# Spreading the first weight loads of a decode block over two hardware DMA queues

## The chip, the cores and the metric

The kernel runs on one core of a Trainium2 chip. The metric is device time in microseconds (us), the median of several executions. Executions of the kernel before agree within about 0.1%, so differences of half a microsecond can be discussed but are near the noise. The profile covers one execution; its span (421.8 us for the kernel before) is about 1.9 us shorter than the measured device time. In the text, MB is 10^6 bytes. The 2048 KB of one K, V or wq load are 2.10 MB, the 1536 KB of one wmod load 1.57 MB. The engines go by their names in the profile: PE multiplies matrices (PEld loads its weights), DVE, ACT and POOL compute on vectors, and SP (SyncE) issues transfers. A load is issued by an engine, waits in a queue, is moved by the DMA engines, and lands when all its bytes are there.

## The reference, cut to what matters

```python
mod = (_silu(c) @ w_mod).reshape(c.shape[0], 6, 1, -1)   # w_mod: 1024 x 6144, 12.6 MB
h = _layernorm(x) * (1 + ca) + sa                        # ca, sa: two of the six parts of mod
q = h @ wq                                               # wq: 1024 x 4096, 8.4 MB
scores = q . k_cache * Dh**-0.5                          # 2 x 4 x 32768 x 128 keys, 67 MB
o = softmax(scores) @ v_cache                            # the same number of values, 67 MB
x = x + ga * (o @ wo)
x = x + gb * MLP(layernorm(x) * (1 + cb) + sb)           # w1, w2, 7.3 MB each; wo is 8.4 MB
```

There are only two rows of x, one per batch. Every weight, key and value is read once: about 178 MB for very little arithmetic per byte.

## The kernel before

All big loads form one ordered list, the stream, and `need(key)` issues it up to the item asked for. SBUF gives the stream a 160 KB ring per partition. Where a load overwrites an older item, its issue waits until the PE has read that item (`frees`):

```python
for k in range(KT8):                                   # 8 slices of w_mod, rows of 12 KB
    add(("wmod", k), [6 * DM], wm_v[:, k, :], k * 12 * KB)
for k in range(4):                                     # 4 loads of wq, rows of 8 KB
    add(("wq", k), [2, HQ * D], ..., (96 + 16 * k) * KB)
for cc in range(4):
    add_kv("K", 0, cc)                                 # K0..K3 of the first of 8 rounds, rows of 16 KB
...                                                    # then V and the next round's K, and so on
def need(*key):
    it = by_key[key]
    while pos[0] <= it.n:
        cur = stream[pos[0]]
        old = [...]                                    # items whose bytes this one overwrites
        ...
        T.dma("sp", lambda e, ...: e.dma_start(dst, src), key=cur.sem, writes=[cur.reg], frees=old)
        pos[0] += 1
    return it
```

`"sp"` is the SyncE instruction stream, so every load goes through that engine's one hardware queue. The start of the kernel is:

```python
need("wmod", 0)
T.dma("sp", ... c2 <- c ...)
T.dma("sp", ... x16 <- A_x ...)
...
for k in range(KT8):                 # PE turns c into columns
    pe(matmul(psM, c2, ident))
act(activation(sgT, cv, ACT.Sigmoid))
...                                  # layernorm of x
for k in range(KT8):
    it = need("wmod", k)             # 12 matmuls for each slice of w_mod
...                                  # modT, modulate
for k in range(KT8):
    it = need("wq", k // 2)          # 8 matmuls for each half of a wq load
...                                  # qT; then the rounds over K and V begin
```

Below, sgT is the sigmoid of c, modT the product with w_mod and qT the query, each turned into columns.

K0 and K1 of the first round overwrite wmod 0 to 2, K2 overwrites wmod 5 and 6, K3 overwrites wq 0. The K0 of the second round overwrites the first round's K0, so it can't be issued before the PE has transposed that tile, and the transposes stand after the q matmuls in the PE's program.

Of the kernel before, what the change touches and what calls it, by code (L numbers as in the profile page):

```python
# [255 lines left out]
def bass_adaLN_cond__gqa_block_cached__mixer_channel_mlp__decode_kernel(  # L256
# [15 lines left out]
    T = Tracker(nc)  # L272
# [133 lines left out]
# [4 lines that stand above are left out]
            old = [o.reg for o in stream[:cur.n] if o.off < cur.off + cur.nbytes and cur.off < o.off + o.nbytes]  # L410
            if len(cur.view.shape) == 3:
                dst = cur.view[:, :, :]
            else:
                dst = cur.view[:, :]
            T.dma("sp", lambda e, dst=dst, src=cur.src: e.dma_start(dst, src), key=cur.sem, writes=[cur.reg], frees=old)  # L415
            pos[0] += 1
        return it

# [7 lines left out]
    def pe(fn, reads=(), writes=(), mark=True):  # L426
        T.inst("pe", fn, reads=reads, writes=writes, mark=mark, sem="pl" if T.lag else None)

    need("wmod", 0)
    T.dma("sp", lambda e: e.dma_start(c2[:, :], c), key="ld_c", writes=["KT_sb0"])  # L430
    T.dma("sp", lambda e: e.dma_start(x16[:, :], A_x.rearrange("b o (k p) -> (b o k) p", p=128)), key="ld_x", writes=["x16"])

    for t, nm in ((ident, "ident"), (identf, "identf")):
        T.inst("pool", lambda e, t=t: e.memset(t[:, :], 0.0), writes=[nm])
# [52 lines left out]
    for k in range(KT8):  # L487
        it = need("wmod", k)
        for ch in range(12):
            n, q = ch // 4, ch % 4  # L490
            pe(lambda e, w=it.view, k=k, ch=ch, n=n, q=q: e.matmul(bank[n][32 * q:32 * q + 32, :], lhsT=inT[:, k, :], rhs=w[:, ch * 512:(ch + 1) * 512],  # L491
                                                                   start=(k == 0), stop=(k == KT8 - 1), skip_group_check=True),
               reads=[it.reg, "inT"], writes=[breg[n]], mark=(ch % 4 == 3))
    for n in range(3):
        dst = row[:, n * 512:(n + 1) * 512]
# [12 lines left out]
    for k in range(KT8):  # L508
        it = need("wq", k // 2)
        for ch in range(8):  # L510
            n, q = ch // 4, ch % 4
            pe(lambda e, w=it.view, k=k, ch=ch, n=n, q=q: e.matmul(bank[n][32 * q:32 * q + 32, :], lhsT=inT[:, k, :], rhs=w[:, k % 2, ch * 512:(ch + 1) * 512],  # L512
                                                                   start=(k == 0), stop=(k == KT8 - 1), skip_group_check=True),
               reads=[it.reg, "inT"], writes=[breg[n]], mark=(ch % 4 == 3))
# [286 lines left out]
```

## Time and profile before

| | kernel before |
|---|---|
| median of device time | 423.67 us (423.66 to 423.82, 3 runs) |
| span of the profile | 421.8 us |
| bytes read | 178.28 MB |
| busy: PE, ACT, DVE | 71%, 37%, 40% |
| first bytes move, last load lands | about 1.5 us, 416.0 us |

From the page of the kernel before: the DMA engines' busy share in forty slices, what they moved, the data queue (packets, MB, share of the 16 engines' span), the bytes read, and the chain that ended last by engine.

```profile
DMA  8999999999999999999999999999999999999995
GB/s 334 429 431 423 435 432 423 429 432 426 433 432 429 435 429 430 435 429 429 435 429 432 437 423 433 435 426 433 433 428 433 430 430 435 427 429 424 428 423 244
...
q1 hardware_dynamic: 14322, 178.29, 99.1%
...
HBM read 178.28 MB, written 0.00 MB: 423 GB/s over the span
...
DMA 80%; PE 16%; ACT 2%; SPq 1%; issue 0%; DVE 0%
```

The rate is flat from the second slice to the last but one, whatever the compute engines do in the meantime. That is the sign of a kernel bound by its bytes. The 80% of DMA in the chain must be read with care. The chain counts a transfer from its issue to its landing, and most of that time is spent in the queue. The view of the K tiles gives that time:

```profile
DMA to landing us min/median/max: 20.2/31.6/35.7
```

A K tile alone takes 2.10 MB / 430 GB/s = 4.9 us (an estimate from the measured rate). So a tile that lands 31.6 us after its issue had some five tiles ahead of it. This is slack: the issue could have come later, and the engines would still have had work.

The timeline of the kernel before, cut to the landmarks at the start (start in us, duration in us, engine, line, operation, output<-input; SPq is SyncE's issuing of loads):

```profile
0.74 0.39 SPq L415 DMA_DIRECT2D wmod<-in_w_mod_dram  x1
...
1.93 3.45 SPq L415 DMA_DIRECT2D wmod<-in_w_mod_dram  x7
...
5.42 16.82 SPq L415 DMA_DIRECT2D wq<-in_A_wq_dram  x4
...
7.60 0.18 ACT L446 ACTIVATE sgT<-psM 128x16 f32<-128x16 f32 x1 [5.59 <-PE psM L444]
...
10.44 1.04 PE L491 MATMUL psS<-wmod,inT 128*32 128x512 bf16 x8
...
22.28 21.50 SPq L415 DMA_DIRECT2D K<-in_A_k_cache_dram  x4
...
40.57 0.26 DVE L506 COPY modT<-psM 128x96 f32<-128x96 f32 x1 [5.38 <-PE psM L503]
...
56.49 0.23 DVE L522 CAST qT<-psM 128x64 bf16<-128x64 f32 x1 [0.54 <-PE psM L519]
...
65.08 11.90 SPq L415 DMA_DIRECT2D K<-in_A_k_cache_dram  x3
```

Seven wmod issues took 3.45 us, but the four wq issues took 16.82 us. Nothing in the program makes wq wait, so the queue itself held SyncE back. The last two lines show the second round: its K0 is issued at 65.08 us, 8.6 us after qT. The windows of the kernel before show that none of this left the DMA engines without work after the first few us. Each line gives the window and its length in us, the busy time (and count of instructions) of PE, PEld, DVE, ACT and POOL, the clock granted to the PE, the busy share of the DMA engines (1 is all of them, all the time) and GB/s:

```profile
0.00:10.00 10.00, 1.33 (x12) 1.18 (x12) 1.20 (x7) 2.75 (x3) 3.34 (x15) 1.00 0.83 329
10.00:50.00 40.00, 22.82 (x170) 9.55 (x170) 3.73 (x14) 0.80 (x2) 0.00 (x0) 1.00 1.01 428
50.00:90.00 40.00, 28.99 (x560) 26.11 (x557) 17.79 (x28) 15.14 (x18) 0.38 (x2) 0.93 1.01 431
```

### The profile page before, as it was taken

Reading aid. Unit: us, or ns where it says so; the run is one execution under the profiler, and the core shown is the slowest. Engines: PE = TensorE matmul, PEld = TensorE weight load, DVE = VectorE, ACT = ScalarE, POOL = GpSimd, SP = SyncE. Lnnn points to the kernel's source line nnn. Section 1 sums busy time; section 2 is a strip of 40 time slices with the busy share of each in tenths; the row PEclk is TensorE's granted clock in tenths of the full one; section 3 lists DMA queues with packets and bytes.
Section 4 is the critical chain, followed back from the end, with each engine's and each line's share of the span. In section 5 each row is a group of like instructions: output and inputs, shape, how many; then the busy total and the mean of one; then the engine's idle time right before and its main releaser. Section 6 shows DMA issues by size and latency. Waiting matters only on the chain.

```text
span 421.8 us, 11638 instructions
## 1 busy us (share of the span) xinstructions
PE 299.5 (71%) x5171; PEld 238.1 (56%) x5171; DVE 167.1 (40%) x347; ACT 156.6 (37%) x269; POOL 6.0 (1%) x31
## 2 busy tenths in 40 slices
PE   1547478878997688587877848796888682445576
PEld 1105158866975678476767828684776671112244
DVE  1102026644663476155534724652474352101311
ACT  2000025547645349142833633383447245000020
POOL 3000000000000000000000000000000000000000
PEclk9999999969989999796988997898899696655565
DMA  8999999999999999999999999999999999999995
GB/s 334 429 431 423 435 432 423 429 432 426 433 432 429 435 429 430 435 429 429 435 429 432 437 423 433 435 426 433 433 428 433 430 430 435 427 429 424 428 423 244
DMA packets 14335, 178.47 MB, mean 423 GB/s; under 512 B 1513, under 2 KB 1520, under 8 KB 2802
## 3 DMA queue, kind: packets, MB, share of 16 engines
q1 hardware_dynamic: 14322, 178.29, 99.1%
q8 instruction: 9, 0.15, 0.1%
q14 instruction: 4, 0.03, 0.0%
HBM read 178.28 MB, written 0.00 MB: 423 GB/s over the span
## 4 chain that ended last, share of the span: by engine, by line
DMA 80%; PE 16%; ACT 2%; SPq 1%; issue 0%; DVE 0%
DMA K<-in_A_k_cache_dram 60%; PE psKT L542 11%; DMA wo<-in_A_wo_dram 8%; DMA w<-in_B_w_dram 7%; DMA wmod<-in_w_mod_dram 4%; PE psS L554 3%; ACT E_sb L575 1%; PE psO L584 1%; SPq L415 1%; ACT KT_sb L546 1%; PE psO L757 1%; PE psS L678 0%; ACT L575 0%; PE psM L565 0%; ACT S_sb L558 0%
## 5 line engine op out<-in xcount | busy, mean ns | idle before, releaser
L542 PE MATMUL psKT<-ident,K 128*128 128x128 bf16 x2048 | 173.8, 237 | 39.0 <-DMA K<-in_A_k_cache_dram 37.8
L542 PEld LDWEIGHTS psKT<-ident,K 128*128 128x128 bf16 x2048 | 133.2, 106 | 49.7 <-DMA K<-in_A_k_cache_dram 44.9
L548 DVE COPY KT_sb<-psKT 128x1024 bf16<-128x1024 bf16 x160 | 108.3, 689 | 112.5 <-PE psKT L542 112.5
L546 ACT ACTIVATE KT_sb<-psKT 128x1024 bf16<-128x1024 bf16 x96 | 98.0, 1020 | 131.2 <-PE psKT L542 131.2
L554 PE MATMUL psS<-qcur,KT_sb 128*128 128x8 bf16 x2048 | 88.2, 167 | 8.1 <-ACT KT_sb L546 6.7
L554 PEld LDWEIGHTS psS<-qcur,KT_sb 128*128 128x128 bf16 x2048 | 79.5, 99 | 13.2 <-ACT KT_sb L546 8.1
L584 PE MATMUL psO<-V,E_sb 128*32 128x512 bf16 x512 | 35.5, 403 | 6.3 <-DMA V<-in_A_v_cache_dram 5.0
L575 ACT ACTIVATE E_sb<-S_sb,negm 128x256 bf16<-128x256 f32 x64 | 32.3, 504 | 7.7 <-DVE negm L571 6.8
L559 DVE TENSOR_REDUCE m1c<-psS 128x8 f32<-128x512 f32 x32 | 22.1, 691 | 14.4 <-ACT S_sb L558 13.3
L558 ACT ACTIVATE S_sb<-psS 128x512 f32<-128x512 f32 x32 | 19.0, 592 | 14.1 <-PE psS L554 14.1
L584 PEld LDWEIGHTS psO<-V,E_sb 128*32 128x32 bf16 x512 | 11.5, 100 | 16.8 <-DMA V<-in_A_v_cache_dram 5.7
L491 PE MATMUL psS<-wmod,inT 128*32 128x512 bf16 x64 | 8.4, 622 | 11.9 <-DMA wmod<-in_w_mod_dram 11.9
L678 PE MATMUL psS<-wo,atT 128*32 128x512 bf16 x64 | 7.6, 627 | 11.3 <-DMA wo<-in_A_wo_dram 11.3
L462 ACT ACTIVATE stat<-stat 128x2 f32<-128x2 f32 x3 | 0.6, 204 | 38.9 <-DVE stat L461 38.9
L512 PE MATMUL psS<-wq,inT 128*32 128x512 bf16 x64 | 7.6, 627 | 6.9 <-DMA wq<-in_A_wq_dram 5.9
L575 ACT ACTIVATION_READ_ACCUMULATOR E_sb<-S_sb,negm 128x1 f32 x64 | 12.1, 189 | 0.0
L491 PEld LDWEIGHTS psS<-wmod,inT 128*32 128x32 bf16 x64 | 1.3, 112 | 17.9 <-DMA wmod<-in_w_mod_dram 17.4
L678 PEld LDWEIGHTS psS<-wo,atT 128*32 128x32 bf16 x64 | 1.9, 128 | 16.3 <-DMA wo<-in_A_wo_dram 10.3
L604 PE MATMUL psM<-msum,hmat 128*128 128x128 f32 x16 | 4.4, 359 | 7.1 <-DVE msum L599 7.1
L497 ACT ACTIVATE S_sb<-psS 128x512 f32<-128x512 f32 x1 | 0.6, 597 | 22.8 <-DVE S_sb L499 22.8
L499 DVE COPY S_sb<-psS 128x512 f32<-128x512 f32 x1 | 0.7, 692 | 20.6 <-PE psS L491 20.6
L599 DVE SCALAR_TENSOR_TENSOR msum<-psO,mk,msum 128x128 f32<-128x128 f32 x24 | 8.4, 351 | 0.8
(116 smaller groups left out, 132.3 us busy)
## 6 DMA issues: line engine op xcount, KB each, us to landing
K<-in_A_k_cache_dram SPq DMA_DIRECT2D x32, 2048.0 KB, 31.6
V<-in_A_v_cache_dram SPq DMA_DIRECT2D x32, 2048.0 KB, 35.1
wmod<-in_w_mod_dram SPq DMA_DIRECT2D x8, 1536.0 KB, 16.5
wq<-in_A_wq_dram SPq DMA_DIRECT2D x4, 2048.0 KB, 37.5
wo<-in_A_wo_dram SPq DMA_DIRECT2D x4, 2048.0 KB, 29.0
w<-in_B_w_dram SPq DMA_DIRECT2D x4, 1792.0 KB, 39.1
w<-in_B_w_dram SPq DMA_DIRECT2D x3, 2048.0 KB, 30.6
w<-in_B_w_dram SPq DMA_DIRECT2D x1, 768.0 KB, 28.0
```

Source lines behind the costliest of these rows:

```text
L491: pe(lambda e, w=it.view, k=k, ch=ch, n=n, q=q: e.matmul(bank[n][32 * q:32 * q + 32, :], lhsT=inT[:, k, :], rhs=w[:, ch * 512:(ch + 1) * 512],
L512: pe(lambda e, w=it.view, k=k, ch=ch, n=n, q=q: e.matmul(bank[n][32 * q:32 * q + 32, :], lhsT=inT[:, k, :], rhs=w[:, k % 2, ch * 512:(ch + ...
L542: pe(lambda e, kq=kq, jj=jj, w=it.view, t=t: e.transpose(psKT[kq][:, jj * 128:(jj + 1) * 128], w[:, t, :], ident[:, :]), reads=[it.reg, "i ...
L546: act(lambda e, src=src: e.activation(KT_sb[g8][:, :, :], src, ACT.Copy), reads=[f"psKT{kq}"], writes=[f"KT_sb{g8}"], sem=f"ev{cc}_{g8}")
L548: dve(lambda e, src=src: e.tensor_copy(KT_sb[g8][:, :, :], src), reads=[f"psKT{kq}"], writes=[f"KT_sb{g8}"], sem=f"ev{cc}_{g8}")
L554: pe(lambda e, t=t, jj=jj: e.matmul(ps[:, t * HPG:(t + 1) * HPG], lhsT=KT_sb[g8][:, jj, :], rhs=qcur[:, :], start=True, stop=True), reads= ...
L558: act(lambda e: e.activation(Sc, ps[:, :].rearrange("p (t h) -> p h t", h=HPG), ACT.Copy), reads=[preg], writes=[f"S_sb{i % 2}_{cc}"], sem ...
L559: dve(lambda e: e.tensor_reduce(m1c[:, :, cc], ps[:, :].rearrange("p (t h) -> p h t", h=HPG), AX.X, ALU.max), reads=[preg], writes=[f"m1c{ ...
L575: act(lambda e: e.activation(E_sb[:, :, h, :], S_sb[j][:, h, :].rearrange("p (u t) -> p u t", t=4), ACT.Exp, bias=negm[:, h:h + 1], scale= ...
L584: pe(lambda e, t4=t4, tg=tg, q=q: e.matmul(psO[32 * q:32 * q + 32, :], lhsT=E_sb[:, tg // 4, :, :].rearrange("p h t -> p (h t)"), rhs=it.v ...
L599: dve(lambda e, q=q: e.scalar_tensor_tensor(out=msum[:, :], in0=psO[:, q * 128:(q + 1) * 128], scalar=mk4[:, q:q + 1], in1=msum[:, :], op0 ...
L678: pe(lambda e, w=it.view, g=g, j=j, hf=hf, q=q: e.matmul(psS[0][32 * q:32 * q + 32, :], lhsT=atT[g][:, j, :], rhs=w[:, j, hf * 512:(hf + 1 ...
```

## The change

The intent is to let two instruction streams issue the first twelve loads: odd slices of wmod and odd loads of wq go through ACT's hardware queue, the others stay on SyncE's. The early call of `need("wq", 3)` puts ACT's six issues at the head of its program, ahead of its sigmoid.

```diff
+            E = "act" if cur.key[0] in ("wmod", "wq") and cur.key[1] % 2 else "sp"
-            T.dma("sp", lambda e, ...: e.dma_start(dst, src), key=cur.sem, ...)
+            T.dma(E, lambda e, ...: e.dma_start(dst, src), key=cur.sem, ...)
...
     need("wmod", 0)
     T.dma("sp", ... c2 <- c ...)
     T.dma("sp", ... x16 <- A_x ...)
+    need("wq", 3)
```

More of the change, by code (lines that the diff above doesn't have):

```diff
@@ L414, in need @@
                 dst = cur.view[:, :]
-            T.dma("sp", lambda e, dst=dst, src=cur.src: e.dma_start(dst, src), key=cur.sem, writes=[cur.reg], frees=old)
+            E = "act" if cur.key[0] in ("wmod", "wq") and cur.key[1] % 2 else "sp"
+            T.dma(E, lambda e, dst=dst, src=cur.src: e.dma_start(dst, src), key=cur.sem, writes=[cur.reg], frees=old)
             pos[0] += 1
```

## The prediction

> **What bounds the kernel now.** The stream of bytes. The page counts 178.28 MB read in a 421.8 us span; its forty slices show the DMA engines 0.9 busy or more in all but the first and the last. In ten-microsecond windows the rate is 420 to 439 GB/s from 10 to 410 us, although PE, ACT and DVE are often half idle. 178.28 MB at 430 GB/s would be 415 us; the rest is the start (nothing moves before 1.5 us; half-microsecond windows show 123, 295, 369 and 393 GB/s from 2 to 4 us, 418 after) and the tail from the last landing (416.0 us). The chain of waits names DMA for 80%, but most of that is queueing: a K tile lands 31.6 us (median) after its issue, never sooner than 20.2 us, V never sooner than 17.9 us, while 2.1 MB at 430 GB/s take 4.9 us (estimate). So 10 us of lateness in an issue costs nothing.
>
> **What the change removes, adds, moves.** Bytes and arithmetic stay. Six issues (wmod 1, 3, 5, 7, wq 1, 3) move from SP to the head of ACT's program.
> - SP's timeline shows about 0.46 us per issue while its queue has room, then 3.07, 6.36 and 6.82 us for wq 1 to 3: back-pressure. These stalls should shrink. They cost nothing today: the engines are full behind them.
> - ACT pays about 6 x 0.46 = 2.8 us at the start, where it only waits for c (5.6 us idle before its sigmoid at 7.6 us). If ACT's queue stalls too, the sigmoid is late but PE catches up: one wmod slice takes it 1.3 us, against 3.65 us to load.
> - Landings: the queues share the engines, so slices should land in pairs. c and x, behind wmod 0, land near 10 us instead of 6.9; first wmod matmul about 13.5 us instead of 10.4. wmod 6 and 7 land together near 32 us; the modT copy moves from 40.6 to about 41.5 us. wq 2 and 3 land together near 53 us; the qT copy moves from 56.5 to about 58.5 us. K0 still lands near 58 us.
>
> The Trainium skill ("DMA: Bandwidth & Descriptors", section "Issuing engines are not separate DMA queues") says loads issued from different engines run on the same 16 DMA engines and interleave, saving only sequencer issue time. The trace of before has one data queue and can't show this.
>
> **How much is critical.** The issue stalls: 0. The lateness of modT and qT: 0, since it delays the issues of K3 (43.5 us now) and of the second round's K0 (65.1 us), each with over 10 us of transfers queued ahead. A fuller start may win: the deficit against 430 GB/s from 1.5 to 4 us is about 0.8 us (estimate from the windows), of which a second queue may fill a quarter. Mixing two queues over 21 MB could change the rate by 1% either way, 0.5 us.
>
> **Predicted: 423.5 us, range 422.7 to 424.4. Chances: faster by over 2% 0.01, within 2% 0.97, slower by over 2% 0.02.**
>
> **What would show the steps.** A second hardware queue with about 10.5 MB, total unchanged; 425 to 435 GB/s from 10 to 50 us; wmod landings in pairs about 7.3 us apart; first wmod matmul 3 us later, modT about 1 us, qT about 2 us later; SP's wq stalls much shorter; K0 lands within 1.5 us of 58 us; from 90 us on both traces agree to about 1 us.
>
> **What would make it wrong.** Two queues mixing clearly below 430 GB/s; one queue served so unfairly that a slice lands 15 us late and K3 is issued into an empty queue; ACT blocked for over 25 us at its issues; a start-up gain above 1 us.

## The result, and the profile after

| | before | after |
|---|---|---|
| median | 423.67 us (423.61 to 423.82, 4 runs) | 423.75 us (423.6 to 423.91, 4 runs) |
| span of the profile | 421.8 us | 421.9 us |
| ratio after / before | | 1.0002, 95% interval 0.9984 to 1.0019 |

A ratio here is the mean time of one kernel's runs over that of the other's of the same rounds, so it isn't quite the ratio of the medians. The time did not change.

The same lines of the page of the changed kernel (q10 is the queue of ACT):

```profile
DMA  8999999999999999999999999999999999999995
GB/s 330 431 429 422 434 433 424 426 433 426 430 437 426 435 432 426 435 435 426 433 433 427 437 428 430 437 426 430 437 426 435 432 427 434 433 424 424 427 426 244
...
q1 hardware_dynamic: 13202, 167.80, 93.3%
q10 hardware_dynamic: 1120, 10.49, 5.9%
...
HBM read 178.28 MB, written 0.00 MB: 423 GB/s over the span
...
DMA 74%; PE 20%; ACT 3%; issue 2%; SPq 1%; DVE 1%; DVEq 0%
```

The second queue, q10, is there with 10.49 MB. The total and the rate are the same. The timeline of the changed kernel (ACTq is ACT's issuing of loads):

```profile
0.73 1.94 ACTq L416 DMA_DIRECT2D wmod<-in_w_mod_dram  x4
...
2.70 1.09 ACTq L416 DMA_DIRECT2D wq<-in_A_wq_dram  x2
...
3.46 1.06 SPq L416 DMA_DIRECT2D wq<-in_A_wq_dram  x2
...
12.21 0.18 ACT L448 ACTIVATE sgT<-psM 128x16 f32<-128x16 f32 x1 [7.10 <-PE psM L446]
...
15.04 1.04 PE L493 MATMUL psS<-wmod,inT 128*32 128x512 bf16 x8
...
17.84 28.30 SPq L416 DMA_DIRECT2D K<-in_A_k_cache_dram  x4
...
42.83 0.26 DVE L508 COPY modT<-psM 128x96 f32<-128x96 f32 x1 [5.38 <-PE psM L505]
...
58.29 0.22 DVE L524 CAST qT<-psM 128x64 bf16<-128x64 f32 x1 [0.55 <-PE psM L521]
...
66.22 12.17 SPq L416 DMA_DIRECT2D K<-in_A_k_cache_dram  x3
```

The issue stalls on wq are gone: 16.82 us for four before, 1.09 and 1.06 us for two and two now. SyncE then issued the first K0 at 17.84 us instead of 22.28, but K0 stood behind the same bytes: by the time from issue to landing of that one load (35.7 us before, 40.2 us now) it landed at 58.0 us in both kernels. In exchange the compute of the start is later: the sigmoid by 4.6 us, the first wmod matmul by 4.6 us, modT by 2.3 us, qT by 1.8 us, the second round's K0 by 1.1 us. The windows of the changed kernel:

```profile
0.00:10.00 10.00, 0.00 (x0) 0.00 (x0) 0.00 (x0) 1.28 (x1) 3.33 (x15) 1.00 0.83 325
10.00:50.00 40.00, 21.81 (x165) 11.17 (x165) 4.92 (x21) 2.27 (x4) 0.00 (x0) 1.00 1.01 428
50.00:90.00 40.00, 30.51 (x587) 26.95 (x588) 18.36 (x31) 15.64 (x18) 0.38 (x2) 0.83 1.01 429
```

The stretch in which two queues mix (10 to 50 us) moved bytes at 428 GB/s in both kernels. The last load's matmuls start at 416.09 us, against 416.02 us before.

### The profile page after: what moved, and what is told of

Its sections match the earlier page's. It is cut to its first block, busy times and chain, and to the rows that moved or that the text cites. A ratio compares the mean times of both kernels' runs of the same rounds, so it can differ in the third digit from the quotient of the medians.

```text
span 421.9 us, 11638 instructions
## 1 busy us (share of the span) xinstructions
PE 298.1 (71%) x5171; PEld 239.6 (57%) x5171; DVE 167.5 (40%) x347; ACT 156.8 (37%) x269; POOL 6.0 (1%) x31
## 3 DMA queue, kind: packets, MB, share of 16 engines
q10 hardware_dynamic: 1120, 10.49, 5.9%
## 4 chain that ended last, share of the span: by engine, by line
DMA 74%; PE 20%; ACT 3%; issue 2%; SPq 1%; DVE 1%; DVEq 0%
DMA K<-in_A_k_cache_dram 47%; PE psKT L544 13%; DMA wq<-in_A_wq_dram 12%; DMA wo<-in_A_wo_dram 8%; DMA w<-in_B_w_dram 7%; PE psS L556 4%; ACT E_sb L577 1%; PE psO L586 1%; SPq L416 1%; ACT KT_sb L548 1%; PE psS L514 1%; PE psO L759 1%; PE psS L680 0%; ACT L577 0%; ACT S_sb L560 0%
## 5 line engine op out<-in xcount | busy, mean ns | idle before, releaser
L586 PE MATMUL psO<-V,E_sb 128*32 128x512 bf16 x512 | 34.6, 396 | 3.6 <-DMA V<-in_A_v_cache_dram 2.1
L561 DVE TENSOR_REDUCE m1c<-psS 128x8 f32<-128x512 f32 x32 | 22.1, 691 | 14.3 <-ACT S_sb L560 13.1
L514 PEld LDWEIGHTS psS<-wq,inT 128*32 128x32 bf16 x64 | 2.4, 139 | 10.8 <-DMA wq<-in_A_wq_dram 6.6
L444 PE MATMUL psM<-ident,KT_sb 2*128 2x2 bf16 x8 | 0.6, 194 | 11.1 <-DMA KT_sb<-in_c_dram 11.1
```

Of the source, the lines that this page charges most:

```text
L514: pe(lambda e, w=it.view, k=k, ch=ch, n=n, q=q: e.matmul(bank[n][32 * q:32 * q + 32, :], lhsT=inT[:, k, :], rhs=w[:, k % 2, ch * 512:(ch + ...
L561: dve(lambda e: e.tensor_reduce(m1c[:, :, cc], ps[:, :].rearrange("p (t h) -> p h t", h=HPG), AX.X, ALU.max), reads=[preg], writes=[f"m1c{ ...
L586: pe(lambda e, t4=t4, tg=tg, q=q: e.matmul(psO[32 * q:32 * q + 32, :], lhsT=E_sb[:, tg // 4, :, :].rearrange("p h t -> p (h t)"), rhs=it.v ...
```

## The experiments

An unchanged time could have three causes, and the trace of one kernel can't tell them apart:

- **Theory A.** The stream of bytes sets the time. It always has work queued, so neither the freed issue stalls nor the later compute reaches it, up to a limit: the engines must never run out of issued loads.
- **Rival B.** Both effects count. The freed stalls win something and the later start of compute loses about as much.
- **Rival C.** A chain of compute sets the time, and the loads only look busy.

There were seven runs of experiment kernels. Every edit below is against the changed kernel. The times are compared with the kernel before, which ran in the same rounds; the changed kernel did not run in them, but takes the same time (423.75 against 423.67 us).

### Fewer bytes, the same arithmetic (e4_drop2)

```diff
-    for k in range(KT8):
+    for k in range(KT8 - 2):
         add(("wmod", k), ...)
...
-        it = need("wmod", k)
+        it = need("wmod", k if k < 6 else k - 2)
```

> Wrong result on purpose: wmod 6 and 7 are not loaded, their matmuls read slices 4 and 5 again. 3.15 MB less to move, the same arithmetic. Theory A (bytes bound the time): 3.15 MB at 430 GB/s = 7.3 us faster, 416.4 us (range 415.8 to 417.0). Rival C (a chain of compute sets the time): less than 1 us faster.

Measured: 416.37 us (416.18 to 416.54) against 423.55 us before, ratio 0.983 (0.9815 to 0.9845). The page counts 175.13 MB. Taking away 3.15 MB won 7.18 us, 439 GB/s at the margin, with the same number of PE matmuls. Theory A expected 7.3 us.

```profile
HBM read 175.13 MB, written 0.00 MB: 423 GB/s over the span
...
50.91 0.23 DVE L524 CAST qT<-psM 128x64 bf16<-128x64 f32 x1 [0.53 <-PE psM L521]
```

The run alone does not refute rival C, though its expectation says so. With two slices fewer, qT came at 50.91 us instead of the changed kernel's 58.29, so a chain of compute that begins at qT would also have ended about as much earlier. Rival C falls by the runs in which compute came later at no cost: modT by 9.7 us and qT by 2.7 us in the next experiment, the sigmoid by 29 us in the one with 12 copies (all against the kernel before). The kernel computes wrong modulation values on purpose. The comparison with the reference is too coarse to see an error of this kind in w_mod.

### More lateness through real traffic (e1_wq_only)

```diff
-            E = "act" if cur.key[0] in ("wmod", "wq") and cur.key[1] % 2 else "sp"
+            E = "act" if cur.key[0] == "wq" and cur.key[1] % 2 else "sp"
```

> Only wq 1 and 3 go to the second queue, at the head of ACT's program; all of wmod stays on SP. They then compete with wmod from the first microsecond, so the last wmod slice should land near 41 us (32 us in the kernel before), modT near 50 us, qT near 60 us: lateness made by real transfers, no stall removed that matters. Theory A (the byte stream is never short of queued work, so lateness within the slack costs nothing): 423.7 us, within 0.5 us of before. Rival B (the change's freed issue stalls and its later modT and qT each count, and cancel): several us slower than before, since the lateness is 4 times that of the change and the stalls freed are no more.

Measured: 423.53 us (423.41 to 423.62) against 423.55 us before, ratio 0.9998 (0.9983 to 1.0013). From its timeline:

```profile
16.08 1.04 PE L493 MATMUL psS<-wmod,inT 128*32 128x512 bf16 x8 [1.53 <-DMA wmod<-in_w_mod_dram]
...
22.45 1.04 PE L493 MATMUL psS<-wmod,inT 128*32 128x512 bf16 x8 [4.90 <-DMA wmod<-in_w_mod_dram]
...
50.27 0.26 DVE L508 COPY modT<-psM 128x96 f32<-128x96 f32 x1 [5.38 <-PE psM L505]
...
59.16 0.22 DVE L524 CAST qT<-psM 128x64 bf16<-128x64 f32 x1 [0.53 <-PE psM L521]
```

modT came at 50.3 us, 9.7 us later than in the kernel before and four times the lateness of the change, at no cost. qT came at 59.2 us, because by then all of wq had landed and the PE only had to catch up. Here SyncE's two wq issues still took 9.86 us together, and that cost nothing either.

### An earlier start of compute (e3_c_first)

```diff
-    need("wmod", 0)
     T.dma("sp", ... c2 <- c ...)
     T.dma("sp", ... x16 <- A_x ...)
+    need("wmod", 0)
     need("wq", 3)
```

> As the changed kernel, but c and x are issued ahead of wmod 0, so the sigmoid no longer waits for wmod 0: c should land near 3 to 4 us instead of 11 us, the first wmod matmul then waits for wmod 0 alone; modT moves only a little (to about 42 us, set by the last pair of slices). Theory A: 423.7 us, within 0.3 us of the changed kernel. Rival B (lateness at the start counts): about 1 us or more faster than the changed kernel.

Measured: 423.61 us (423.53 to 423.77) against 423.55 us before, ratio 1.0 (0.9986 to 1.0014). The sigmoid ran at 6.7 us instead of 12.2 us. modT did not follow: it came at 43.5 us, where 42 was expected, because the last pair of wmod slices sets it. So this run undid the lateness of the sigmoid only. It agrees with theory A but tells less than planned.

### How much lateness is free (e5_delay12, e7_delay18, e6_delay24)

Dummy copies on ACT stand between the transposes of c and the sigmoid. They write a buffer that is overwritten later.

```diff
+    for n in range(12):      # 18 and 24 in the other two
+        act(lambda e: e.activation(S_sb[1] as 128x2048, onesf broadcast, ACT.Copy), ...)
     act(lambda e: e.activation(sgT[:, :, :], cv, ACT.Sigmoid), ...)
```

> The changed kernel with 12 dummy ACT copies of 128x2048 elements between the transposes of c and the sigmoid, about 1.9 us each (estimate from 592 ns for 512 and 1020 ns for 1024 elements), 23 us in all. modT should move from 42.8 to about 56 us, qT from 58.3 to about 66 us, K3's issue to about 58 us, the second round's K0 to about 74 us; wq, K0 to K2, K3, V0 and V1 keep the engines fed until about 81 us. Theory A: no more than 0.5 us slower than before. Rival B (lateness at the start counts one for one or in part): 4 to 14 us slower.

Measured with 12 copies: 423.66 us (423.6 to 423.8) against 423.71 us before, ratio 1.0 (0.9983 to 1.0016). From the timeline of that run:

```profile
36.60 0.18 ACT L451 ACTIVATE sgT<-psM 128x16 f32<-128x16 f32 x1
...
42.23 13.18 SPq L416 DMA_DIRECT2D K<-in_A_k_cache_dram  x4
...
60.27 0.23 DVE L527 CAST qT<-psM 128x64 bf16<-128x64 f32 x1 [0.53 <-PE psM L524]
...
65.62 15.23 SPq L416 DMA_DIRECT2D K<-in_A_k_cache_dram  x3
```

The sigmoid ran 24.4 us later than in the changed kernel, and the first K0 was issued 24.4 us later. qT moved by only 2.0 us, to 60.3 us: all wmod slices had landed, and all of wq by the time the PE came to it, so the PE ran through them without waiting. The second round's K0 did not come later at all. The lateness was used up in the slack. It also means that this run delayed only the first round's K0. The second round's K0 was issued between 65 and 67 us in every run so far that moved all the bytes, so its own slack is not measured by these delays; the run with all loads on one queue, below, shows its end.

> The same with 24 copies, about 45 us. Now the wmod matmuls start only near 60 us, so K0 is issued near 62 us while wq ended at about 51 us, and the queue runs dry, then again before K3. Theory A: 12 to 20 us slower than before (about 440 us), with DMA shares well under 1 between 52 and 64 us; the sudden step from nothing at 23 us to many us at 45 us is what a queue with slack gives. Rival B: 10 to 35 us slower, in proportion to the 23 us run.

Measured with 24 copies: 439.98 us (439.63 to 441.4), ratio 1.0381 (1.0364 to 1.0398). K0 was issued at 65.4 us, and the windows of that run show the empty queue:

```profile
40.00:51.00 11.00, 0.00 (x0) 0.00 (x0) 0.00 (x0) 10.81 (x7) 0.00 (x0) 1.00 1.01 429
51.00:67.00 16.00, 5.46 (x48) 2.69 (x52) 2.76 (x15) 10.35 (x8) 0.00 (x0) 1.00 0.08 22
```

Between 51 and 67 us the engines moved 22 GB/s. At 430 GB/s that is 16 x (430 - 22) / 430 = 15.2 us of lost transfer. The execution that was profiled took 441.4 us, the longest of the four and 17.7 us over the median of before (16.3 us between the medians). Of the 2.5 us left, 1.7 us lie in windows that moved less than 430 GB/s (401 from 67 to 77 us, 401 and 413 from 100 to 120 us). The second dry spell that was expected before K3 did not come: K3 was issued at 78.35 us, and the engines moved 430 GB/s from 77 to 90 us.

> The delay again, with 18 copies, to place the edge of the slack from numbers of the two earlier delays. 12 copies put the sigmoid at 36.6 us and the first issue of K0 at 42.2 us, 24 copies at 59.8 and 65.4 us: 1.93 us per copy, so 18 copies should give 48.2 and 53.8 us. The wq loads end at about 51.4 us (the 24-copy run went dry there), and data flows about 0.8 us after an issue, so the engines should stand empty for about 3.2 us and never again. Theory A: 426.9 us, between 426.2 and 428.0. A cost proportional to the delay (half of what 24 copies cost) would be about 8 us: 432 us; none at all, 423.7 us.

Measured with 18 copies: 428.88 us (428.23 to 430.08) against 423.65 us before, ratio 1.0133 (1.0113 to 1.0153). The sigmoid came at 48.23 us and K0's issue at 53.87 us, as calculated. The cost of 5.2 us lies above the stated range of 426.2 to 428.0 us and clearly below the 432 us of a cost in proportion. The windows of that run:

```profile
51.00:58.00 7.00, 7.00 (x85) 2.85 (x89) 1.56 (x8) 0.20 (x1) 0.00 (x0) 1.00 0.54 170
58.00:90.00 32.00, 25.76 (x439) 20.89 (x428) 12.71 (x23) 10.15 (x12) 0.19 (x1) 0.84 1.01 428
```

The loss in the first line is 7 x (430 - 170) / 430 = 4.2 us. The execution that was profiled took 428.23 us, 4.6 us over the median of before. What the calculation had left out is the way back to full rate. In windows of 2 us the engines moved 156 GB/s from 54 to 56 us and 360 from 56 to 58 us, so the restart cost about 1 us beyond the gap itself (an estimate from these windows). The four executions spread over 1.85 us, where those of the kernel before spread over 0.30 us. One profile can't tell why; that stays open.

Together the three delays show the form of slack: nothing at 24 us of lateness, 5 us at 36 us, 16 us at 48 us (the sigmoid against that of the changed kernel, 12.21 us). From 36 to 48 us the sigmoid moved by 11.6 us and the time by 11.1 us, almost one for one. A share of every lateness, as rival B has it, would have cost many us at the first step.

### Everything on the second queue (e2_all_act)

```diff
-            E = "act" if cur.key[0] in ("wmod", "wq") and cur.key[1] % 2 else "sp"
+            E = "act" if cur.key[0] in ("wmod", "wq") else "sp"
```

> All twelve wmod and wq loads on ACT's queue, SP keeps c, x and the K and V tiles. ACT should meet the back-pressure that SP shows in the kernel before, so its sigmoid waits until about 22 us, and K0 to K2, then K3, V0 and V1, compete with wq from about 27 us on, so wq 3 lands between 70 and 85 us and the first round's transposes start after it. Theory A with its limit: the queue then holds nothing more to move at about 80 us (33.6 MB at 430 GB/s) while the second round's K0 can be issued only near 83 to 90 us: 4 to 13 us slower than before, with DMA idle in windows around 80 to 92 us. Rival B': any split over two queues is free whatever the order: 423.7 us.

Measured: 440.63 us (439.82 to 441.91) against 423.55 us before, ratio 1.041 (1.0391 to 1.0428). This is the one split that hurt, 17.1 us, and more than the 4 to 13 us expected. Its timeline:

```profile
4.71 17.79 ACTq L416 DMA_DIRECT2D wq<-in_A_wq_dram  x4
...
23.82 0.18 ACT L448 ACTIVATE sgT<-psM 128x16 f32<-128x16 f32 x1
...
59.06 1.90 PE L514 MATMUL psS<-wq,inT 128*32 128x512 bf16 x16 [11.95 <-DMA wq<-in_A_wq_dram]
...
73.12 1.90 PE L514 MATMUL psS<-wq,inT 128*32 128x512 bf16 x16 [12.16 <-DMA wq<-in_A_wq_dram]
...
85.64 0.23 DVE L524 CAST qT<-psM 128x64 bf16<-128x64 f32 x1 [0.54 <-PE psM L521]
...
92.89 10.93 SPq L416 DMA_DIRECT2D K<-in_A_k_cache_dram  x3
```

and its windows:

```profile
60.00:80.00 20.00, 2.86 (x28) 0.51 (x20) 0.00 (x0) 0.00 (x0) 0.00 (x0) 0.50 1.00 425
80.00:94.00 14.00, 9.87 (x153) 8.37 (x154) 4.74 (x8) 3.67 (x4) 0.19 (x1) 0.62 0.09 27
```

ACT did meet the back-pressure (17.79 us for four issues, like SyncE's 16.82 us before), and its sigmoid waited for that until 23.8 us. This was harmless: the 12-copy delay ran its sigmoid at 36.6 us for nothing, and modT came at 39.6 us here, earlier than in the changed kernel. The damage came after it. One wq load of 2.10 MB took 73.12 - 59.06 = 14.06 us to follow the one before it, 149 GB/s of some 425: a third. K and V tiles on the other queue took the rest. The packet counts of the queues fit one packet per row: q10 of the changed kernel counts 1120 packets, which is 4 x 128 rows of wmod, 2 x 256 rows of wq and 16 more for each of the six loads. A wq row has 8 KB and a K or V row 16 KB. If the engines take a packet from each queue in turn, wq gets one third of the bytes. The counts of q10 in this run (2240) and in the wq-only run (544) fit one packet per row too. The Trainium skill ("DMA: Bandwidth & Descriptors", section "Queues, rings and completion order") says that each engine goes round between the queues with work at the granularity of a packet; this trace agrees, with 149 GB/s against about 276. That the packets of the profile are those that take turns is an inference. The wq-only run gives a second look, less clear. There wmod slices (rows of 12 KB) ran beside wq (rows of 8 KB), so turns by packet would give wmod 60% and an even split by bytes 50%. Slice 2 came 22.45 - 16.08 = 6.37 us after slice 1, which is 247 GB/s of 434: 57%. Slice 1, with the small loads of c and x ahead of it, had come 7.2 us after slice 0 (by their times from issue to landing): 51%. No run varied the length of the rows alone.

So K and V tiles that nobody could use yet passed in front of the wq loads that everything waited for. qT came at 85.6 us. The second round's K0 was issued at 92.89 us, but the engines had finished all that had been issued at about 80.5 us. They stood nearly idle from 80 to 94 us: 14 x (430 - 27) / 430 = 13.1 us, and the climb back (374 GB/s from 94 to 110 us) adds 16 x (430 - 374) / 430 = 2.1 us. That accounts for 15.2 of the 16.5 us by which the profiled execution was longer (440.08 us). The rest was not sorted out.

No experiment with all the bytes gave a version that beats the kernel before, and none pointed to one: the DMA engines were busy throughout from 10 to 400 us (share 1.01, 430 GB/s), in both kernels.

## Why the prediction was right

- **The bound.** Right. Bytes set the time: 3.15 MB less won 7.18 us with the same matmuls, and compute that came later cost nothing as long as the engines had issued loads.
- **The freed issue stalls are worth nothing.** Right. wq's stalls went from 16.82 us to about 2 us, and the time stayed. In the wq-only run 9.86 us of stall remained, and the time was the same too. No run freed the stalls without moving any compute.
- **The later compute costs nothing, with over 10 us of slack.** Right, and the slack was understated. The sigmoid could come 24.4 us later for nothing; at 36 us the queue ran dry. The prediction took its 10 us from the shortest time from issue to landing (20.2 and 17.9 us). The delays measured the slack at the start itself: the first K0 has to be issued before the last wq bytes are moved, near 51 us.
- **The lateness itself.** The mechanism was right and the sizes were too small. The sigmoid's input c was put near 10 us and came at 11.1; x came later still (the PE's turning of x into columns, for which the sigmoid waits in this program, started at 11.98 us), so the first wmod matmul was at 15.0 us, not 13.5. modT moved by 2.3 us, not 1: the last pair of slices arrived together at 33.45 us, 1 us later than the last single slice before (32.47 us), and the PE had two slices left to do after it. qT was right, 58.3 us against 58.5 predicted.
- **K0.** Right. It was to land within 1.5 us of 58 us, and landed at 58.0 us.
- **Pairs.** Right. The PE waited for wmod at 19.27, 26.61 and 33.45 us only, each time for two slices; the steps are 7.34 and 6.84 us (7.3 predicted).
- **A fuller start might win 0.2 us.** Wrong, though far inside the range. The first 10 us moved 325 GB/s against 329: a second queue did not fill the climb to full rate.
- **The traces agree to 1 us from 90 us on.** Wrong as stated. The K0 of the third round was issued 1.4 us earlier than in the kernel before (93.16 against 94.52 us), that of the fourth 2.4 us earlier (123.08 against 125.44); the fifth agreed (161.38 against 161.41). The rate from 90 to 400 us is 431 GB/s in both kernels, so these shifts stayed within the slack too.
- **What would make it wrong.** The case that the prediction named, a queue served so unfairly that issues come into an empty queue, is real: the run with all loads on ACT's queue is that case, at 17.1 us, only that there the second round's K0 came too late and not K3. The alternating split escapes it, as far as these runs show, because each queue has wmod beside wmod and wq beside wq, and both queues have as many bytes ahead of K0; no run tested this reason by itself.

The skill's statement that the prediction leaned on (the same page, section "Issuing engines are not separate DMA queues") is borne out by the changed kernel: 428 GB/s from 10 to 50 us with one queue and with two.

## What to carry to other kernels

When the DMA engines are already full, moving issues to a second engine changes only the order in which data lands, and the stalls in the issuing timeline are a sign of a full queue, not a loss. Find how late the next issue may come before the engines run out of issued work; inside that slack lateness is free, beyond it nearly every us counts (11.1 of 11.6 here). If two queues must share the engines, keep loads that nothing needs yet out of the queue that runs beside the urgent ones, above all when their rows are longer.

## What the Trainium skill lacked or had wrong

- "DMA: Bandwidth & Descriptors", section "Queues, rings and completion order", gives the round by packets but not what it seems to mean for two loads on two queues: that the share goes with the length of the rows. wq with 8 KB rows got 149 of about 425 GB/s beside K and V with 16 KB rows. One pair of row lengths showed this clearly, a second (12 KB beside 8 KB, 51% and 57%) less so.
- The same page, "Rules for kernel authors", says that spreading loads over issuing engines doesn't help bandwidth. The runs agree (428 GB/s both ways), but the page lacks the warning that it can hurt: moving all twelve loads to the second queue cost 17.1 us through the order of landing.
- The same page treats back-pressure for remote transfers only. Local loads show it too: with twelve big loads on one queue the last four issues held SyncE for 16.82 us, and ACT for 17.79 us; with six on each queue nothing was held.
- No page has the cost of restarting a queue that ran empty. After the gap of the 18-copy run, the 2 us windows moved 156 and 360 GB/s before the full rate came back, about 1 us beyond the gap.
- The same page, section "Where 436 GB/s comes from", says that for transfers between HBM and SBUF the HBM side of about 358 GB/s binds. Here one core alone held 428 to 431 GB/s for 390 us, which fits that page's own single-core measurement of 425 GB/s rather than the sentence.
